# The first microseconds of a linear-attention and SwiGLU kernel: tile 0's mean in two halves on two engines, a split weight load, and a new order of the first tiles

## The chip, the cores and the metric

The kernel runs on one core of a Trainium2 chip. The metric is device time in microseconds (us). The core's engines are TensorE (PE, with its weight loads shown as PEld), VectorE (DVE), ScalarE (ACT), GpSimd (POOL) and SyncE (SP, which here only issues DMAs). Each engine runs its own instructions in order and waits on semaphores for the others.

## The reference

x has 2048 rows of 512 columns in bfloat16. The output is x plus two branches of the same normalised x:

```python
xn = _layernorm(x, axis=-1)                # (x - mean) / sqrt(var + 1e-5), per row
return x + _A_ref(xn, wqkv, wo) + _B_ref(xn, w_gate, w_up, w_down)
# A: q, k, v = xn @ wqkv, 32 heads of 16
#    phi(t) = where(t > 0, t + 1, exp(t)) + 1e-6
#    kv = phi(k)^T v ; z = sum over rows of phi(k)
#    o = phi(q) kv / (phi(q) z + 1e-6) ; o @ wo
# B: (silu(xn @ w_gate) * (xn @ w_up)) @ w_down, 1792 wide
```

## The kernel before, in words

The 2048 rows are 16 tiles of 128 rows (t = 0 to 15). Three stages follow one another on PE: the projections of K and Q with the outer product of xn and phi(K) for all tiles (some 50 us), then the gate and up projections of the feed-forward part with the attention's small matrices between them, then the output tiles.

The order of the work is written out by hand. `K.op(engine, ...)` appends an instruction to an engine's list with the names that it reads and writes; the helper class `_Prog` turns these into semaphore waits. The order of the calls from line 608 on is therefore the order in each engine's queue. DMAs go out on SP's queue (`xload`, L204, tiles of x; `wqkv_load`, L211, blocks of 128 rows of K's or Q's weights, 128 KB each) and two of them on ACT's queue: x of tile 1 and K's block 3.

The head works as follows. PE runs eight matmuls on constants (`fill`, L269) that only keep it busy. For tile 0, DVE takes mean and variance (`bns`, L297, and `agg`, L300), then centres x in two halves of 256 columns (`xc_half`, L380). For tile 1 the mean alone comes from ACT, which copies x times 1/512 with an accumulator (`mean_act`, L305); for tile 2 it comes from `bns` and `agg`. PE transposes the centred blocks of 128 columns (`tp_first`, L408) into PSUM, two to a bank, and ACT copies them to `xcT` (`tc_first`, L420). Then PE projects block by block (`proj_part`, L463, and `proj_first`, L450): a tile's K needs four blocks c of `xcT`, each with the weight block c. Tile 3 is transposed by DMA (`transpose_xc`, L399), tiles 4 and up from xn.

The first tiles are centred but not scaled. The scale 1/sqrt(var+eps) (`rstd`, made on POOL by `eps`, L325, and `rstd_of`, L334) goes in when ACT reads the projections from PSUM: `first_ek` (L520, exponential of K), `first_pk` (L526, positive part of K), `first_pq` (L538, Q). `clip_k` (L503) on DVE and `feat_pool` (L545, POOL) or `first_feat` (L552, DVE) finish phi(K). The outer product `gtacc` (L588) needs phi(K) and xn of the tile; xn comes from DVE (`xn_dve`, L314).

PSUM has eight banks. K of tile t goes to bank 2(t%2), Q to bank 2(t%2)+1, so tile 2 needs tile 0's banks back, and tile 3 those of tile 1: K3 waits for `first_ek(1)` and `first_pk(1)`, Q3 for `first_pq(1)`. The constants' matmuls use bank 3, the transposes of tiles 0 and 1 banks 4 to 7, which `gtacc` takes over.

A matmul's waits are set by the names it reads. One `proj_part` reads one block:

```python
r=[("xcT", t, c // 2), (wname, c)], w=[bk(b)],
```

Of the kernel before, what the change touches and what calls it, by code (L numbers as in the profile page):

```python
# [6 lines left out]
ACT = mybir.ActivationFunctionType  # L7
ALU = mybir.AluOpType
AX = mybir.AxisListType

P = 128
S = 2048
D = 512
# [4 lines left out]
NDC = D // P  # L18
# [90 lines left out]
def bass_parallel_sum__linear_attn_block__swiglu_ffn__prompt_kernel(  # L109
# [12 lines left out]
    K = _Prog()  # L122
    pe, act, dve, pool, sp = nc.tensor, nc.scalar, nc.vector, nc.gpsimd, nc.sync
    bf, f32 = dt.bfloat16, dt.float32

    with contextlib.ExitStack() as es:
        E = es.enter_context

        def sb(name, shape, d=bf):
            return E(nc.sbuf_tensor(name, [P] + shape, d))  # L130

        x_sb = sb("x_sb", [NT, D])
        xn_sb = sb("xn_sb", [NT, D])
        xc_sb = sb("xc_sb", [4, D])
        xcT = sb("xcT", [4 * NDC, P])
# [7 lines left out]
        ident = sb("ident", [P])  # L143
# [3 lines left out]
        mv = sb("mv", [NT, 2], f32)  # L147
        vpe = sb("vpe", [NT], f32)
        rstd = sb("rstd", [NT], f32)
# [4 lines left out]
        warm = sb("warm", [1], f32)  # L154
        mact = sb("mact", [2, 1], f32)
        scr = sb("scr", [D])
        pkq = sb("pkq", [NT, 2, D])
        zacc = sb("zacc", [D], f32)
        zhi = sb("zhi", [D])
# [30 lines left out]
        def bk(i):  # L190
            return ("bank", i)
# [16 lines left out]
        def wqkv_load(eng, h, name, i, c0, n, after=()):  # L208
            K.dma(
                eng,  # L210
                lambda: h.dma_start(  # L211
                    wqkv_sb[:, c0:c0 + n, i * D:(i + 1) * D],
                    A_wqkv[c0 * P:(c0 + n) * P, i * D:(i + 1) * D].rearrange("(c p) f -> p c f", p=P),
                ),
                r=list(after), w=[(name, c) for c in range(c0, c0 + n)],
            )
# [29 lines left out]
        K.op("pool", lambda: pool.memset(nhalf[:, :], -0.5), w=[("nhalf",)])  # L246

        xload("sp", sp, 0, 1)
        wqkv_load("sp", sp, "wk", 1, 0, 2)
        wqkv_load("act", act, "wk", 1, 3, 1)  # L250
        wqkv_load("sp", sp, "wk", 1, 2, 1)
        xload("sp", sp, 2, 1)
# [12 lines left out]
        def fill(n, cols, after=()):  # L265
            K.op(
                "pe",
                [
                    (lambda: pe.matmul(banks[3][:, 0:cols], cw, cx[:, 0:cols], start=True, stop=True))  # L269
                    for _ in range(n)  # L270
                ],
                r=list(after), w=[bk(3)],
            )
# [22 lines left out]
        def bns(t):  # L296
            K.op("dve", lambda: dve.bn_stats(stats[:, t, :], x_sb[:, t, :]), r=[("x", t)], w=[("st", t)])  # L297

        def agg(t):
            K.op("dve", lambda: dve.bn_aggr(mv[:, t, :], stats[:, t, :]), r=[("st", t)], w=[("mv", t)])  # L300

        def mean_act(t):
            K.op(
                "act",
                lambda: act.activation(  # L305
                    scr[:, :], x_sb[:, t, :], ACT.Copy, scale=1.0 / D, accum_out=mact[:, t, :],
                ),
                r=[("x", t)], w=[("mact", t), ("scr",)],
            )

        def xn_dve(t):
            K.op(
                "dve",
                lambda: dve.tensor_scalar(  # L314
                    out=xn_sb[:, t, :], in0=x_sb[:, t, :], scalar1=mv[:, t, 0:1], scalar2=rstd[:, t:t + 1],
                    op0=ALU.subtract, op1=ALU.mult,
                ),
                r=[("x", t), ("mv", t), ("rstd", t)], w=[("xn", t)],
            )

        def eps(t, eng):
            h = dve if eng == "dve" else pool
            K.op(
                eng,
                lambda: h.tensor_scalar(  # L325
                    out=vpe[:, t:t + 1], in0=mv[:, t, 1:2], scalar1=1e-5, scalar2=None, op0=ALU.add,
                ),
                r=[("mv", t)], w=[("vpe", t)],
            )

        def rstd_of(t):
            K.op(
                "pool",
                lambda: pool.tensor_tensor(out=rstd[:, t:t + 1], in0=vpe[:, t:t + 1], in1=nhalf[:, 0:1], op=ALU.pow),  # L334
                r=[("vpe", t), ("nhalf",)], w=[("rstd", t)],
            )
# [35 lines left out]

        HD = D // 2

        def xc_half(t, h, mean=None, dep="mv"):
            mean = mv[:, t, 0:1] if mean is None else mean

            K.op(
                "dve",
                lambda: dve.tensor_scalar(  # L380
                    out=xc_sb[:, t, h * HD:(h + 1) * HD], in0=x_sb[:, t, h * HD:(h + 1) * HD],
                    scalar1=mean, scalar2=None, op0=ALU.subtract,
                ),
                r=[("x", t), (dep, t)], w=[("xc", t, h)],
            )

        def xc_full(t):
            K.op(
                "dve",
                lambda: dve.tensor_scalar(  # L390
                    out=xc_sb[:, t, :], in0=x_sb[:, t, :], scalar1=mv[:, t, 0:1], scalar2=None, op0=ALU.subtract,
                ),
                r=[("x", t), ("mv", t)], w=[("xc", t, 0), ("xc", t, 1)],
            )

        def transpose_xc(t):
# [6 lines left out]
        def tp_first(t, h, b):  # L403
            tb = banks[b].bitcast(bf)[:, 0:HD].rearrange("p (c s) -> p c s", c=2)
            K.op(
                "pe",
                [
                    (lambda c=c: pe.transpose(  # L408
                        tb[:, c, :], xc_sb[:, t, (2 * h + c) * P:(2 * h + c + 1) * P], ident[:, :],
                    ))  # L410
                    for c in range(2)
                ],
                r=[("xc", t, h), ("ident",)], w=[bk(b)],
            )

        def tc_first(t, h, b):
            tb = banks[b].bitcast(bf)[:, 0:HD].rearrange("p (c s) -> p c s", c=2)
            K.op(
                "act",
                lambda: act.activation(xcT[:, NDC * t + 2 * h:NDC * t + 2 * h + 2, :], tb, ACT.Copy),  # L420
                r=[bk(b)], w=[("xcT", t, h)],
            )

        def transpose_dma(t):
# [34 lines left out]
        def proj_part(t, wname, c, pos):  # L459
            lo, b = (D, kb(t)) if wname == "wk" else (0, qb(t))  # L460
            K.op(
                "pe",
                lambda: pe.matmul(  # L463
                    banks[b], xcT[:, NDC * t + c, :], wqkv_sb[:, c, lo:lo + D],
                    start=(pos == 0), stop=(pos == NDC - 1),
                ),
                r=[("xcT", t, c // 2), (wname, c)], w=[bk(b)],
            )

        def kb(t):  # L470
# [47 lines left out]
        def first_ek(t):  # L518
            K.op(
                "act", lambda: act.activation(ek[:, t % NE, :], banks[kb(t)], ACT.Exp, scale=rstd[:, t:t + 1]),  # L520
                r=[bk(kb(t)), ("rstd", t)], w=[("ek", t % NE)],
            )

        def first_pk(t):
            K.op(
                "act", lambda: act.activation(kpos[:, t % NE, :], banks[kb(t)], ACT.Relu, scale=rstd[:, t:t + 1]),  # L526
                r=[bk(kb(t)), ("rstd", t)], w=[("kpos", t % NE)],
            )
# [7 lines left out]
        def first_pq(t):  # L536
            K.op(
                "act", lambda: act.activation(pkq[:, t, 1, :], banks[qb(t)], ACT.Identity, scale=rstd[:, t:t + 1]),  # L538
                r=[bk(qb(t)), ("rstd", t)], w=[("pq", t)],
            )  # L540
# [15 lines left out]
        def clip_k(t):  # L556
            clip(ek[:, t % NE, :], ("ek", t % NE))
# [47 lines left out]
            if t >= 3:  # L605
                transpose_dma(t)

        fill(8, 512)
        bns(0)
        agg(0)  # L610
        xc_half(0, 0)
        xc_half(0, 1)
        mean_act(1)
        xc_half(1, 0, mact[:, 1, :], "mact")
        xc_half(1, 1, mact[:, 1, :], "mact")
        tp_first(0, 0, 4)
        tc_first(0, 0, 4)
        fill(1, P)
        tp_first(0, 1, 5)
        tc_first(0, 1, 5)  # L620
        eps(0, "pool")
        tp_first(1, 0, 6)
        tc_first(1, 0, 6)
        bns(1)
        rstd_of(0)
        xn_dve(0)
        tp_first(1, 1, 7)
        agg(1)
        tc_first(1, 1, 7)
        bns(2)  # L630
        agg(2)
        xc_half(2, 0)
        xc_half(2, 1)
        bns(3)
        agg(3)
        proj_part(0, "wk", 0, 0)
        proj_part(0, "wk", 1, 1)
        proj_part(0, "wk", 3, 2)
        proj_part(0, "wk", 2, 3)
        first_ek(0)  # L640
        clip_k(0)
        xc_full(3)
        bns(4)
        proj_part(1, "wk", 0, 0)
        proj_part(1, "wk", 1, 1)
# [6 lines left out]
        xload("sp", sp, 10, 2)  # L652
        proj_part(0, "wq", 0, 0)
        proj_part(0, "wq", 1, 1)
        first_pk(0)
        tp_first(2, 0, 4)
        tc_first(2, 0, 4)
        tp_first(2, 1, 5)
# [7 lines left out]
        proj_part(1, "wq", 2, 2)  # L666
        proj_part(0, "wq", 3, 3)
        first_pq(0)
        proj_part(1, "wq", 3, 3)
        proj_first(2, "wk", 0)  # L670
        proj_first(2, "wk", 1)
        eps_two(1, "pool")
        rstd_two(1)
        first_ek(1)
        clip_k(1)
        first_pq(1)
        proj_first(2, "wq", 0)
# [7 lines left out]
        xn(4)  # L685
        xload("sp", sp, 12, 2)
        xn_dve(1)
        first_pk(1)
        first_feat(1)
        proj_first(3, "wk", 0)  # L690
        first_ek(2)
# [371 lines left out]
```

## Time and profile before

| | |
|---|---|
| time, median of 3 runs | 211.19 us (210.76 to 211.28) |
| the profiled execution | 211.17 us |
| its span | 209.9 us, 2767 instructions |
| PE busy | 207.3 us, 99% of the span |
| DVE, ACT, POOL busy | 119.5, 70.9, 72.0 us |
| chain that ended last | PE 99% |
| granted TensorE clock | 1.0 |

The span runs from the first to the last instruction of the profiled execution; its own time is 1.27 us longer. Times in the views are counted from the span's start. A line of a timeline gives start and length in us, the engine, the line of the kernel, the operation, what it writes and reads, how many instructions are merged in it, and in brackets how long the engine stood idle before and what ended that. A busy PE is not a PE at its peak: ends of matmuls are modelled and overlap, so the distance between starts tells the rate.

### The profile page before, as it was taken

To read this page: it belongs to the slowest core of one execution; us is meant where nothing else is said; L and a number is where in the kernel's file an instruction comes from. 1 tells how busy PE (TensorE), PEld (TensorE's weight loads), DVE (VectorE), ACT (ScalarE), POOL (GpSimd) and SP (SyncE) were. 2 spreads that over 40 slices of the span, in tenths; PEclk is the share of its full clock that TensorE was granted. 3 is DMA by queue.
4 is the path that set the end of the run, shared out by engine and by line. 5 is a ranking of instruction groups with operands and counts; after the bars stand their busy time and mean duration, and the time that the engine had idled before them with its cause. 6 is when DMAs were issued, how large, how long until landed. Compare 5 with 4: busy or idle time off the path is not lost.

```text
span 209.9 us, 2767 instructions
## 1 busy us (share of the span) xinstructions
PE 207.3 (99%) x987; PEld 95.3 (45%) x987; DVE 119.5 (57%) x245; ACT 70.9 (34%) x125; POOL 72.0 (34%) x90
## 2 busy tenths in 40 slices
PE   8999999999999999999999999999999999999996
PEld 3444444445444444444444444444444444444444
DVE  4989988336265774647365746365556535374122
ACT  5787666966643331302122312213031213121000
POOL 3527977568032444222141432230424032221200
PEclk9999999999999999999999999999999999999999
DMA  6773744894792011110202110202021010210201
GB/s 192 228 192 66 127 100 100 260 365 153 206 352 47 11 28 26 34 25 28 50 2 50 25 28 25 50 0 50 3 50 25 27 25 28 44 33 27 50 25 53
DMA packets 30287, 16.84 MB, mean 80 GB/s; under 512 B 20928, under 2 KB 29632, under 8 KB 30272
## 3 DMA queue, kind: packets, MB, share of 16 engines
q1 hardware_dynamic: 29984, 16.39, 29.6%
q10 hardware_dynamic: 288, 0.26, 0.4%
q8 instruction: 8, 0.13, 0.3%
q14 instruction: 7, 0.06, 0.1%
HBM read 9.70 MB, written 2.10 MB: 56 GB/s over the span
## 4 chain that ended last, share of the span: by engine, by line
PE 99%; DVE 0%; issue 0%
PE psum L783 46%; PE psum L966 23%; PE psum L436 10%; PE psum L955 7%; PE psum L588 7%; PE psum L463 2%; PE psum L269 2%; PE psum L450 2%; PE psum L408 1%; PE psum L881 0%; PE psum L904 0%; DVE out_sb L979 0%
## 5 line engine op out<-in xcount | busy, mean ns | idle before, releaser
L798 ACT ACTIVATE sg<-psum 128x512 bf16<-128x512 f32 x56 | 33.4, 598 | 106.8 <-PE psum L783 104.9
L783 PE MATMUL psum<-xnT,wu_sb 128*128 128x512 bf16 x224 | 57.5, 379 | 0.0
L783 PE MATMUL psum<-xnT,wg_sb 128*128 128x512 bf16 x224 | 57.5, 379 | 0.0
L913 POOL TENSOR_TENSOR prod<-pkq,zb 128x512 f32<-128x512 bf16 x16 | 18.6, 1162 | 57.7 <-DVE pkq L512 57.7
L783 PEld LDWEIGHTS psum<-xnT,wu_sb 128*128 128x128 bf16 x224 | 21.9, 98 | 26.4
L783 PEld LDWEIGHTS psum<-xnT,wg_sb 128*128 128x128 bf16 x224 | 21.9, 98 | 26.2
L979 DVE TENSOR_TENSOR out_sb<-psum,x_sb 128x512 bf16<-128x512 f32 (+2 forms) x17 | 11.2, 660 | 36.3 <-PE psum L966 36.3
L804 DVE TENSOR_TENSOR pkq<-psum,sg 128x512 bf16<-128x512 f32 x28 | 19.2, 687 | 18.5 <-PE psum L783 14.0
L937 POOL TENSOR_TENSOR pqn<-pkq,rden 128x512 bf16<-128x512 bf16 x16 | 16.9, 1057 | 36.6 <-DVE rden L931 36.6
L804 DVE TENSOR_TENSOR xn_sb<-psum,sg 128x512 bf16<-128x512 f32 x28 | 18.8, 673 | 13.8 <-PE psum L783 13.2
L966 PE MATMUL psum<-wd_sb,xn_sb 128*128 128x512 bf16 (+2 forms) x126 | 25.7, 355 | 0.0
L966 PE MATMUL psum<-wd_sb,pkq 128*128 128x512 bf16 x112 | 25.5, 379 | 0.0
L436 PE MATMUL psum<-wqkv_sb,xnT 128*128 128x512 bf16 x96 | 22.5, 379 | 0.0
L580 POOL TENSOR_TENSOR zacc<-zacc,pkq 128x512 f32<-128x512 f32 x15 | 17.3, 1156 | 5.0 <-DVE ek L503 4.6
L966 PEld LDWEIGHTS psum<-wd_sb,xn_sb 128*128 128x128 bf16 x126 | 11.8, 98 | 12.5
L966 PEld LDWEIGHTS psum<-wd_sb,pkq 128*128 128x128 bf16 x112 | 11.0, 98 | 13.2
L955 PE MATMUL psum<-m_sb,eq 128*128 128x512 bf16 (+2 forms) x68 | 16.6, 366 | 0.0
L588 PE MATMUL psum<-pkq,xn_sb 128*128 128x512 bf16 x64 | 15.9, 379 | 0.0
L436 PEld LDWEIGHTS psum<-wqkv_sb,xnT 128*128 128x128 bf16 x96 | 9.4, 98 | 11.3
L921 DVE TENSOR_REDUCE den<-prod 128x32 f32<-128x512 f32 x16 | 10.9, 684 | 5.7 <-POOL prod L913 5.7
L297 DVE BATCH_NORM_STATS2 stats<-x_sb 128x6 f32<-128x512 bf16 x16 | 10.9, 681 | 3.2 <-DMA x_sb<-in_A_x_dram 3.0
L512 DVE SCALAR_TENSOR_TENSOR pkq<-pkq,eq 128x512 bf16<-128x512 bf16 x16 | 11.1, 692 | 0.6
(67 smaller groups left out, 139.6 us busy)
## 6 DMA issues: line engine op xcount, KB each, us to landing
out_dram<-out_sb SPq DMA_DIRECT2D x15, 128.0 KB, 1.7
wg_sb<-in_B_w_gate_dram SPq DMA_DIRECT2D x2, 896.0 KB, 7.8
wu_sb<-in_B_w_up_dram SPq DMA_DIRECT2D x2, 896.0 KB, 6.1
wd_sb<-in_B_w_down_dram SPq DMA_DIRECT2D x1, 1792.0 KB, 9.9
x_sb<-in_A_x_dram SPq DMA_DIRECT2D x5, 256.0 KB, 3.1
x_sb<-in_A_x_dram SPq DMA_DIRECT2D x5, 128.0 KB, 3.5
wqkv_sb<-in_A_wqkv_dram SPq DMA_DIRECT2D x5, 128.0 KB, 3.6
wqkv_sb<-in_A_wqkv_dram SPq DMA_DIRECT2D x1, 512.0 KB, 7.8
```

The costliest lines, as they stand in the source:

```text
L436: (lambda c=c: pe.matmul(banks[b], xnT[:, c, t * P:(t + 1) * P], wqkv_sb[:, c, lo:lo + D], start=(c == 0), stop=(c == NDC - 1),))
L512: lambda: dve.scalar_tensor_tensor(out=dst, in0=src, scalar=0.0, in1=e, op0=ALU.max, op1=ALU.add,),
L580: lambda: pool.tensor_tensor(out=zacc[:, :], in0=zacc[:, :], in1=pk, op=ALU.add),
L588: (lambda c=c: pe.matmul(banks[4 + c], xn_sb[:, t, c * P:(c + 1) * P], pkq[:, t, 0, :], start=(t == 0), stop=(t == NT - 1),))
L783: (lambda c=c: pe.matmul(banks[b], w_sb[:, c, fc * P:(fc + 1) * P], xnT[:, c, C * 512:(C + 1) * 512], start=(c == 0), stop=(c == NDC - 1),))
L798: lambda: act.activation(sg[:, j % NSG, :], banks[gb], ACT.Silu),
L804: lambda: dve.tensor_tensor(out=hT(C, fc), in0=banks[ub], in1=sg[:, j % NSG, :], op=ALU.mult,),
L913: lambda: pool.tensor_tensor(out=p, in0=pkq[:, t, 1, :], in1=zb[:, :], op=ALU.mult),
L937: lambda: pool.tensor_tensor(out=pqn[:, t % NPN, :].rearrange("p (h e) -> p h e", e=DH), in0=pkq[:, t, 1, :].rearrange("p (h e) -> p h e", ...
L955: (lambda g=g: pe.matmul(dst, pqnT(t)[:, g, :], m_sb[:, g, lo:hi], start=(g == 0), stop=False,))
L966: (lambda fc=fc: pe.matmul(dst, hT(C, fc)[:, jj * P:(jj + 1) * P], wd_sb[:, fc, lo:hi], start=False, stop=(fc == NFC - 1),))
L979: lambda: dve.tensor_tensor(out=o, in0=src, in1=x_sb[:, t, lo:hi], op=ALU.add),
```

## The change

Six things change, all in the first part of the order.

1. Tile 0's mean comes from two halves: DVE multiplies columns 0 to 255 by ones and sums them, ACT copies columns 256 to 511 with its accumulator (`mean_parts`). DVE subtracts both parts in one instruction per half tile (`xc_two`). `bns(0)` and `agg(0)` follow behind.
2. The first two transposes of tile 0 go to banks of their own (4 and 1), with a copy of 128 columns each (`tp_quarter`, `tc_quarter`).
3. K's weight blocks 0 and 1 come in two loads of 128 KB instead of one of 256 KB, both on SP.
4. The constants' matmuls are seven of 512 columns, one of 128, and later two of 128 where one was. Tile 1's transposes move behind the first two projections of tile 0.
5. Tiles 1 and 2 are centred in one instruction (`xc_full`). Tile 3's centring moves ahead of `clip_k(0)`.
6. Tile 0 is normalised on ACT (`xn_act`, with a bias from POOL's `negmean`) behind `first_pq(0)`; its eps goes from POOL to DVE; `first_pk(0)` and `first_pk(1)` move up behind `first_ek`.

The core of the diff:

```diff
-        wqkv_load("sp", sp, "wk", 1, 0, 2)
+        wqkv_load("sp", sp, "wk", 1, 0, 1)
+        wqkv_load("sp", sp, "wk", 1, 1, 1)
...
+        def negmean(t):
+            K.op(
+                "pool",
+                lambda: pool.tensor_scalar(
+                    out=nb[:, t:t + 1], in0=mv[:, t, 0:1], scalar1=rstd[:, t:t + 1], scalar2=-1.0,
+                    op0=ALU.mult, op1=ALU.mult,
+                ),
+                r=[("mv", t), ("rstd", t)], w=[("nb", t)],
+            )
+
+        def xn_act(t):
+            K.op(
+                "act",
+                lambda: act.activation(
+                    xn_sb[:, t, :], x_sb[:, t, :], ACT.Identity, scale=rstd[:, t:t + 1], bias=nb[:, t:t + 1],
+                ),
+                r=[("x", t), ("nb", t), ("rstd", t)], w=[("xn", t)],
+            )
...
+        def mean_parts(t):
+            K.op(
+                "dve",
+                lambda: dve.tensor_tensor_reduce(
+                    out=scr2[:, :], in0=x_sb[:, t, 0:HD], in1=cx[:, 0:HD], scale=1.0 / D, scalar=0.0,
+                    op0=ALU.mult, op1=ALU.add, accum_out=mpart[:, 0:1],
+                ),
+                r=[("x", t)], w=[("mpa", t), ("scr2",)],
+            )
+            K.op(
+                "act",
+                lambda: act.activation(
+                    scr[:, 0:HD], x_sb[:, t, HD:D], ACT.Copy, scale=1.0 / D, accum_out=mpart[:, 1:2],
+                ),
+                r=[("x", t)], w=[("mpb", t), ("scr",)],
+            )
+
+        def xc_two(t, h):
             K.op(
                 "dve",
                 lambda: dve.tensor_scalar(
                     out=xc_sb[:, t, h * HD:(h + 1) * HD], in0=x_sb[:, t, h * HD:(h + 1) * HD],
+                    scalar1=mpart[:, 0:1], scalar2=mpart[:, 1:2], op0=ALU.subtract, op1=ALU.subtract,
+                ),
+                r=[("x", t), ("mpa", t), ("mpb", t)], w=[("xc", t, h)],
+            )
...
+        def xct_res(t, c):
+            return ("xcT", 0, "b") if (t, c) == (0, 1) else ("xcT", t, c // 2)
+
+        def tp_quarter(t, c, b):
+            K.op(
+                "pe",
+                lambda: pe.transpose(
+                    banks[b].bitcast(bf)[:, 0:P], xc_sb[:, t, c * P:(c + 1) * P], ident[:, :],
+                ),
+                r=[("xc", t, 0), ("ident",)], w=[bk(b)],
+            )
+
+        def tc_quarter(t, c, b):
+            K.op(
+                "act",
+                lambda: act.activation(xcT[:, NDC * t + c, :], banks[b].bitcast(bf)[:, 0:P], ACT.Copy),
+                r=[bk(b)], w=[xct_res(t, c)],
+            )
...
-        fill(8, 512)
+        fill(7, 512)
+        fill(1, P)
+        mean_parts(0)
+        mean_act(1)
+        xc_two(0, 0)
+        xc_two(0, 1)
         bns(0)
+        xc_full(1, mact[:, 1, :], "mact")
         agg(0)
-        xc_half(0, 0)
-        xc_half(0, 1)
-        mean_act(1)
-        xc_half(1, 0, mact[:, 1, :], "mact")
-        xc_half(1, 1, mact[:, 1, :], "mact")
-        tp_first(0, 0, 4)
-        tc_first(0, 0, 4)
-        fill(1, P)
+        eps(0, "dve")
+        rstd_of(0)
+        negmean(0)
+        tp_quarter(0, 0, 4)
+        tc_quarter(0, 0, 4)
+        tp_quarter(0, 1, 1)
+        tc_quarter(0, 1, 1)
         tp_first(0, 1, 5)
         tc_first(0, 1, 5)
-        eps(0, "pool")
-        tp_first(1, 0, 6)
-        tc_first(1, 0, 6)
+        fill(2, P)
         bns(1)
-        rstd_of(0)
-        xn_dve(0)
-        tp_first(1, 1, 7)
         agg(1)
-        tc_first(1, 1, 7)
         bns(2)
         agg(2)
-        xc_half(2, 0)
-        xc_half(2, 1)
+        xc_full(2)
         bns(3)
         agg(3)
         proj_part(0, "wk", 0, 0)
         proj_part(0, "wk", 1, 1)
+        tp_first(1, 0, 6)
+        tc_first(1, 0, 6)
+        tp_first(1, 1, 7)
+        tc_first(1, 1, 7)
         proj_part(0, "wk", 3, 2)
         proj_part(0, "wk", 2, 3)
+        xc_full(3)
         first_ek(0)
+        first_pk(0)
         clip_k(0)
-        xc_full(3)
         bns(4)
...
-        first_pk(0)
...
         first_pq(0)
+        xn_act(0)
...
         first_ek(1)
+        first_pk(1)
         clip_k(1)
         first_pq(1)
...
-        first_pk(1)
```

More of the change, by code (lines that the diff above doesn't have):

```diff
@@ L156, in bass_parallel_sum__linear_attn_block__swiglu_ffn__prompt_kernel @@
         scr = sb("scr", [D])
+        scr2 = sb("scr2", [D // 2])
+        mpart = sb("mpart", [2], f32)
         pkq = sb("pkq", [NT, 2, D])
@@ L373, in bass_parallel_sum__linear_attn_block__swiglu_ffn__prompt_kernel, with xc_full @@
         HD = D // 2
-        def xc_half(t, h, mean=None, dep="mv"):
+        def mean_parts(t):
[16 more added lines that the diff above has]
+            K.op(
+                "dve",
+                lambda: dve.tensor_scalar(
+                    out=xc_sb[:, t, h * HD:(h + 1) * HD], in0=x_sb[:, t, h * HD:(h + 1) * HD],
+                    scalar1=mpart[:, 0:1], scalar2=mpart[:, 1:2], op0=ALU.subtract, op1=ALU.subtract,
+                ),
+                r=[("x", t), ("mpa", t), ("mpb", t)], w=[("xc", t, h)],
+            )
+        def xc_full(t, mean=None, dep="mv"):
             mean = mv[:, t, 0:1] if mean is None else mean
@@ L380, in xc_half @@
                 lambda: dve.tensor_scalar(
-                    out=xc_sb[:, t, h * HD:(h + 1) * HD], in0=x_sb[:, t, h * HD:(h + 1) * HD],
-                    scalar1=mean, scalar2=None, op0=ALU.subtract,
-                ),
[L384 to L393, printed above, removed]
+                    out=xc_sb[:, t, :], in0=x_sb[:, t, :], scalar1=mean, scalar2=None, op0=ALU.subtract,
+                ),
+                r=[("x", t), (dep, t)], w=[("xc", t, 0), ("xc", t, 1)],
             )
@@ L421, in tc_first @@
                 r=[bk(b)], w=[("xcT", t, h)],
+            )
[10 more added lines that the diff above has]
+        def tc_quarter(t, c, b):
+            K.op(
+                "act",
+                lambda: act.activation(xcT[:, NDC * t + c, :], banks[b].bitcast(bf)[:, 0:P], ACT.Copy),
+                r=[bk(b)], w=[xct_res(t, c)],
             )
@@ L466, in proj_part @@
                 ),
-                r=[("xcT", t, c // 2), (wname, c)], w=[bk(b)],
+                r=[xct_res(t, c), (wname, c)], w=[bk(b)],
             )
```

## The prediction

> **What bounds the kernel now.** I read the page first: TensorE (PE) is busy 99% of the 209.9 us span, and part 4 puts 99% of the chain that ended last on PE. The change touches only the first 13 us, so next I read the chain of waits in order of time, cut to its start (columns: start, length, what).
>
> ```profile
> 0.84 3.57 PE psum L269 x8
> 4.41 0.32 PE psum L408 x2
> 4.73 0.11 PE psum L269
> 4.84 0.64 PE psum L408 x6
> 5.48 2.90 PE psum L463 x12
> 8.37 0.22 PE psum L408 x4
> 8.59 0.86 PE psum L463 x4
> 9.46 1.73 PE psum L450 x8
> ```
>
> The reader sees PE without a gap from the first warming matmul (L269) on. From the first transpose (L408, 4.33) PE does useful work back to back. So a microsecond is won only if this useful work starts earlier or has less to do, and lost wherever PE has to wait.
>
> Second, the spacing of matmuls. 512 columns take 0.427 us before about 6 us (2.93, 3.35, 3.78 in the timeline of L269) and 0.216 after (2.90 us for 12 has one and a half slow ones). The same change shows in the view of line L463:
>
> ```profile
> L463 PE MATMUL psum<-wqkv_sb,xcT x16: 379/379/634, 5.3 to 9.1; 128*128 128x512 bf16 x16
> ```
>
> One matmul of 634 ns is at half rate. The matmuls start at 5.27, 5.70 and 6.05: the second took 0.35, and half rate for x, full rate for 0.35-x, gives 1.2x + 2.4(0.35-x) = 0.512, x = 0.27. So PE stepped to full rate at about 5.97.
>
> Third, the timelines of VectorE (DVE) and ScalarE (ACT) say what releases the first transposes and projections:
>
> ```profile
> 3.04 0.69 DVE L297 BATCH_NORM_STATS2 stats<-x_sb 128x6 f32<-128x512 bf16 x1 [3.04 <-DMA x_sb<-in_A_x_dram]
> 3.77 0.18 DVE L300 BATCH_NORM_AGGREGATE mv<-stats 128x2 f32<-128x6 f32 x1
> 3.99 0.48 DVE L380 TENSOR_SCALAR xc_sb<-x_sb,mv 128x256 bf16<-128x256 bf16 x2
> ...
> 3.35 0.63 ACT L305 ACTIVATE scr<-x_sb 128x512 bf16<-128x512 bf16 x1 [1.05 <-DMA x_sb<-in_A_x_dram]
> 3.88 0.19 ACT L305 ACTIVATION_READ_ACCUMULATOR scr<-x_sb 128x1 f32 x1
> 4.77 1.25 ACT L420 ACTIVATE xcT<-psum 128x256 bf16<-128x256 bf16 x4 [0.69 <-PE psum L408]
> ```
>
> x of tile 0 lands at 3.04, its centred first half starts at 3.99, PE starts on it at 4.33, ACT copies from 4.77 to 5.15, and the first K matmul runs at 5.27.
>
> **The change part by part.**
>
> **1. Mean of tile 0 in halves.** Removed from the path: bn_stats 0.69 + aggregate 0.18 and their gaps, 3.04 to 3.99. Added on ACT: a 256-column copy with accumulator. The 512-column row is 0.629; 256 columns less cost 0.215 on ACT (PSUM copies: 598 and 383 ns), so 0.415, then the accumulator read of 0.186, which starts 0.10 before the end: 3.04+0.415-0.10+0.186 = 3.54. Added on DVE: a reducing two-tensor operation on 256 columns, which no row shows. Two-tensor rows of 128, 384 and 512 columns (L979: 292, 558, 692 ns) give 0.425 for 256. Whether it needs a read of its own is unknown: 0 to 0.186, by ACT's row. At worst the whole is as slow as a 512-wide reduction (L921, 684 ns) plus that read. I take 0.425+0.15, hence 3.61, and 0.04 for the own-engine wait: centring starts at 3.65 (bounds 3.58 and 3.95) instead of 3.99. Its two scalars cost 0.05 more (two-scalar L314 0.400, one-scalar L390 0.347): 0.33. First half ready 3.98, PE 4.04 (4.33 before). The warming matmuls, one of 512 exchanged for one of 128, end at 0.84+7x0.427+0.107 = 3.94, and the identity at 3.84, so neither delays it.
>
> **2. Quarters.** A transpose ends 0.29 after its start and ACT follows 0.04 later: 4.37. A 128-column copy is 0.383-0.107 = 0.276, ending 4.65; from a copy's end to the matmul it was 0.12 (5.15 to 5.27). First K matmul at 4.77, **0.50 earlier**. Second copy ends 4.83, so the second K matmul follows at 5.20, if its weights are there.
>
> **3. What PE does with it.** Tile 1's four transposes, which stood ahead of K0 (4.63 to 5.05), now stand behind its second matmul. Still at half rate: K0's first two 4.77 to 5.62, transposes from 5.62 (0.107 each); the step at 5.97 comes in the fourth; K0's last two 6.02 and 6.23, end 6.45. But the first copy of tile 1 now starts only at 5.73+0.31+0.04 = 6.08 and ends 6.46, so K1 starts at 6.58. Before it was 5.27+0.43+0.35+2x0.216 = 6.48. **The head start of 0.50 is gone: +0.10.** The moved transposes, the half rate and the added 128-column filler eat 0.47 of it (6.45 against 6.48), and the wait for the copy costs 0.13.
>
> On the clock the row comes first: full rate began 5.1 us after the first matmul. The Trainium skill, "TensorE: Matmul & The Clock Gate", Part 1, says PE runs at half rate until about 3.4 us of sustained activity have filled a window that runs free of the kernel. By that rule work moved ahead of the step earns half of its time later, which is against this change; were there no such step, the sum at K1 would be a gain of about 0.2 us. The matmul spacings above agree with it.
>
> **4. K's blocks 0 and 1 in two loads.** One more issue of 0.43 on SP; everything behind it on SP's queue moves: block 2 of K, x of tile 2, four of Q, x of 3 to 7. In the view of DMA issues the loads take longer than they need when alone:
>
> ```profile
> wqkv_sb<-in_A_wqkv_dram SPq DMA_DIRECT2D x1, 256.0 KB, 2.9
> ...
> wqkv_sb<-in_A_wqkv_dram ACTq DMA_DIRECT2D x1, 128.0 KB, 3.7
> ```
>
> 256 KB issued at 1.26 landed at 4.16; x of tile 0, first in line, took 2.2, ACT's block 3 landed at 5.19, SP's block 2 (1.73+3.9) at 5.63, tile 2 (2.23+3.8) at 6.03. DMA busy share is 0.9 to 1.0 from 2 to 7 us, so later issues mostly shorten the queueing: shifts lie between 0 and 0.43. Needed against landing: block 1 at 5.20, issued 1.69, lands 3.9 (+2.2) to 5.2 (block 3's time); I take 4.6. Block 2 at 6.23 against 5.63 to 6.06. Tile 2 at most 6.46; DVE then centres it by 7.75, needed by its transposes at 8.21. Q's first, 2.71+3.6 = 6.3, at most 6.75, needed at 7.34. Cost taken: 0, hidden by these slacks; if block 1 comes with block 2, see rivals.
>
> **5. Tiles 1 and 2 whole, tile 0 normalised on ACT.** One 512-wide centring is 0.347 against 0.48 for two halves: DVE only, off the path. DVE loses 0.40 (L314) and gains 0.15 (eps); bn_stats of tile 0 moves behind centring, so rstd(0) comes at 6.1 instead of 5.1, still ahead of exp of K0 at 6.7. xc(3) and clip(0) swap: clip(0) ends about 9.2, POOL's 1.16 us then gives pk(0) at 10.4, needed by the outer product at 11.02. The added ACT pass (L538's kind, 0.69) ends at 10.56: in time too. But ACT is a full queue here:
>
> ```profile
> 9.28 0.69 ACT L538 ACTIVATE pkq<-psum,rstd 128x512 bf16<-128x512 f32 x1
> 9.87 0.68 ACT L520 ACTIVATE ek<-psum,rstd 128x512 bf16<-128x512 f32 x1
> 10.44 0.69 ACT L538 ACTIVATE pkq<-psum,rstd 128x512 bf16<-128x512 f32 x1
> 11.01 0.70 ACT L526 ACTIVATE kpos<-psum,rstd 128x512 f32<-128x512 f32 x1
> ```
>
> The step is 0.573. With the new pass second, and pk(1) ahead of pq(1), the order is pq0, xn0, ek1, pk1, pq1. pk1, which frees K3's bank, still ends at 11.71, but pq1, which frees Q3's bank, ends at 9.28+4x0.573+0.69 = 12.27, and PE wants that bank at 11.88+2x0.216 = 12.31. With 0.04 to 0.13 from release to matmul, Q3 starts near 12.41: **+0.10**. Behind that ACT has 0.42 of idle time before 13.86, which takes up the remaining 0.57 late by then.
>
> **Sum.** +0.10 (K1) +0.10 (Q3) = +0.20 on the profiled execution (211.17: span 209.9 and 1.27 around it), 0.02 under the median of 211.19. Forecast **211.4**, its own range 211.0 to 211.8. A difference of 0.3%, 0.63 us, is about what a measurement of this kernel can tell from no change.
>
> **Rivals.**
> *The head start survives.* If PE steps to full rate before 4.3, the 0.50 is carried on; if DVE needs no accumulator read, 0.07 more: 210.6. Against it: 5.97 in this execution, and K0's last block lands at 5.63 at the earliest, where K0 ends at 6.48 now. For it: the three times before spread by 0.52, as a step that moves would do. Between, 210.9.
> *Block 1's load is late.* It decides from a landing at 5.15. With block 2's 5.63, the second matmul runs at 5.70 to 6.05, transposes follow, the copy ends at 6.75, K1 starts at 6.87: +0.39, with Q3's 0.10 gives 211.7; with 0.43 more on block 2 of K and tile 2 up to 212.1. For it: block 3 itself took 3.7.
> *Slower by the clock.* PE now idles from 4.68 to 4.77 and, with a late block 1, up to 0.6 us around 5.2. If that gap starts the count to full rate anew, the 5.1 us begin at 5.3 and half rate lasts to 10.4 instead of 5.97: half of 4.4 us is lost, 213.4. It decides at the first gap too long. The gap of 0.07 before 4.33 did no harm. That page's rule, that the window runs free, speaks for 1.7 at most.
>
> **Chances.** Forecast 0.54, head start 0.22, late block 0.16, clock 0.08. Faster by over 0.3% only at the far end of the head start, 0.12; slower: the clock 0.08, half of the late block 0.08, 0.06 of the forecast's high end (a slow reduction and a late tile 2 together): 0.22; the same 0.66. The range 210.6 to 212.2 leaves out the clock and the tails.
>
> **What would show it.** First K matmul near 4.77; ACT's first copy of tile 1 at 6.08; K1 at 6.58; an idle PE before Q3 on ACT's L538; the step to 0.216 near 6. Wrong would be: K1 well under 6.4, a wait of PE on a weight DMA near 5.2, or half rate past 7.

## The result and the profile after

The changed kernel takes 211.43 us (median of 22 runs, 211.04 to 211.77), the kernel before 210.93 (22 runs beside them, 210.49 to 211.56). The ratio is **1.0022, 95% interval 1.0014 to 1.0030**: slower by 0.46 us (0.30 to 0.63). The profiled execution of the changed kernel took 211.42 (span 210.2), that of the kernel before 211.17.

First the chain of waits of the changed kernel, cut to its start (start, length, what). L520 is `proj_part`, L507 `proj_first`, L446 the transposes, L645 `gtacc`, L595 `first_pq`, L327 the new pass for xn, L577 `first_ek`, L583 `first_pk`. K0 stands for the projection of K of tile 0, Q3 for that of Q of tile 3, and so on; K1 "at 6.55" is the start of its first matmul.

```profile
1.72 3.73 DMA wqkv_sb<-in_A_wqkv_dram
5.45 0.14 issue
5.59 0.38 PE psum L520
5.96 0.22 PE psum L446 x4
6.19 2.27 PE psum L520 x10
...
9.36 0.69 ACT pkq L595
10.05 0.70 ACT xn_sb L327
10.75 0.58 ACT ek L577
11.33 0.59 ACT kpos L583
11.92 0.05 issue
11.97 2.04 PE psum L507 x8
14.01 1.73 PE psum L645 x8
```

Before, this chain was PE alone. Now it starts at a weight load: K's block 1, issued on SP at 1.72, lands at 5.45, and the second matmul of K0 waits for it. Later it runs through ScalarE's queue. The eight matmuls from 11.97 (K3 and Q3) take 2.04, where the same number takes 1.73 elsewhere; part of that is how the view merges, and the starts give the wait. The changed kernel, on PE and among PE's weight loads (PEld), then the kernel before:

```profile
11.97 2.04 PE L507 MATMUL psum<-wqkv_sb,xcT 128*128 128x512 bf16 x8
13.85 0.38 PE L645 MATMUL psum<-pkq,xn_sb 128*128 128x512 bf16 x1
12.54 0.98 PEld L507 LDWEIGHTS psum<-wqkv_sb,xcT 128*128 128x128 bf16 x6 [0.47 <-ACT pkq L595]
```

```profile
11.88 1.89 PE L450 MATMUL psum<-wqkv_sb,xcT 128*128 128x512 bf16 x8
13.61 0.38 PE L588 MATMUL psum<-pkq,xn_sb 128*128 128x512 bf16 x1
```

From K3's start to gtacc(1) it is 11.97 to 13.85, 1.88; before it was 11.88 to 13.61, 1.73. So **0.15 is lost before Q3**, whose weight load waits for ScalarE's first_pq(1).

PE's timeline around the first wait:

```profile
4.57 0.61 PE L520 MATMUL psum<-wqkv_sb,xcT 128*128 128x512 bf16 x1
5.59 0.38 PE L520 MATMUL psum<-wqkv_sb,xcT 128*128 128x512 bf16 x1 [0.41 <-DMA wqkv_sb<-in_A_wqkv_dram]
```

The first K matmul runs at 4.57, 0.70 earlier than before; the second at 5.59, 0.11 earlier. K1 starts at 6.55 (6.48 before), K2 at 9.38 (9.29), gtacc(1) at 13.85 (13.61). The distance of 0.23 to 0.24 stays to the end: the last output tile's 14 matmuls start at 207.39 against 207.15.

The head itself, on VectorE and ScalarE:

```profile
2.85 0.42 DVE L400 CUSTOM_DVE_ANT_0 scr<-x_sb,const-bfloat16-1.0 128x256 bf16<-128x256 bf16 x1 [2.85 <-DMA x_sb<-in_A_x_dram]
3.20 0.08 DVE L400 DVE_READ_ACCUMULATOR2_ANT mpart<- 128x1 f32 x1
3.40 0.64 DVE L417 TENSOR_SCALAR xc_sb<-x_sb,mpart 128x256 bf16<-128x256 bf16 x2
```

```profile
2.85 0.42 ACT L408 ACTIVATE scr<-x_sb 128x256 bf16<-128x256 bf16 x1 [0.55 <-DMA x_sb<-in_A_x_dram]
3.17 0.19 ACT L408 ACTIVATION_READ_ACCUMULATOR scr<-x_sb 128x1 f32 x1
...
9.95 0.80 ACT L327 ACTIVATE xn_sb<-x_sb,nb,rstd 128x512 bf16<-128x512 bf16 x1
```

Both halves of the mean are there 0.51 after x lands (x itself was there 0.19 earlier, at 2.85 instead of 3.04; over the profiles below VectorE starts on it between 2.85 and 3.23), and centring starts 0.55 after it, where it took 0.95. The new pass on ScalarE is the longest of its row: it takes 0.80, and its successor starts 0.70 after it, not 0.57.

### The profile page after: what moved, and what is told of

Same layout as the page of the kernel before. It is cut to its first block, busy times and chain, and to the rows that moved or that the text cites. A ratio compares the mean times of both kernels' runs of the same rounds, so it can differ in the third digit from the quotient of the medians.

```text
span 210.2 us, 2760 instructions
## 1 busy us (share of the span) xinstructions
PE 206.1 (98%) x969; PEld 94.9 (45%) x988; DVE 119.8 (57%) x245; ACT 72.0 (34%) x129; POOL 72.0 (34%) x90
## 4 chain that ended last, share of the span: by engine, by line
PE 95%; DMA 2%; ACT 1%; issue 1%; SPq 0%; DVE 0%
PE psum L843 46%; PE psum L1026 23%; PE psum L493 10%; PE psum L1015 6%; PE psum L645 6%; DMA wqkv_sb<-in_A_wqkv_dram 2%; PE psum L520 2%; PE psum L507 1%; PE psum L941 0%; PE psum L964 0%; ACT xn_sb L327 0%; ACT pkq L595 0%; ACT kpos L583 0%; ACT ek L577 0%; PE psum L446 0%
## 5 line engine op out<-in xcount | busy, mean ns | idle before, releaser
L843 PE MATMUL psum<-xnT,wg_sb 128*128 128x512 bf16 x215 | 55.9, 379 | 0.1
L1015 PE MATMUL psum<-m_sb,eq 128*128 128x512 bf16 (+2 forms) x65 | 16.1, 366 | 0.1
L645 PE MATMUL psum<-pkq,xn_sb 128*128 128x512 bf16 x61 | 15.5, 379 | 0.1
```

The costliest lines, as they stand in the source:

```text
L645: (lambda c=c: pe.matmul(banks[4 + c], xn_sb[:, t, c * P:(c + 1) * P], pkq[:, t, 0, :], start=(t == 0), stop=(t == NT - 1),))
L843: (lambda c=c: pe.matmul(banks[b], w_sb[:, c, fc * P:(fc + 1) * P], xnT[:, c, C * 512:(C + 1) * 512], start=(c == 0), stop=(c == NDC - 1),))
L1015: (lambda g=g: pe.matmul(dst, pqnT(t)[:, g, :], m_sb[:, g, lo:hi], start=(g == 0), stop=False,))
```

## The experiments

**Theory and rivals after the result.** Theory: two waits belong to the change, block 1's load near 5.2 and ScalarE's pass before Q3. Rivals: one of them costs nothing by itself; or the difference is only PE's step to full rate, which may fall anywhere. The first two runs undo one part each, the third undoes both, and the fourth puts the split load alone into the kernel before.

**e1: one load for blocks 0 and 1.**

```diff
-        wqkv_load("sp", sp, "wk", 1, 0, 1)
-        wqkv_load("sp", sp, "wk", 1, 1, 1)
+        wqkv_load("sp", sp, "wk", 1, 0, 2)
```

> The changed kernel with K's blocks 0 and 1 in one load of 256 KB again. Theory (two waits: 0.41 us of PE idle on block 1's load near 5.2, and 0.15 us before Q3 on ScalarE): no wait of PE on a weight DMA, second K matmul by 5.2 instead of 5.59, K1 at about 6.40 instead of 6.55, the wait before Q3 stays; 0.15 under the changed kernel, ratio to before about 1.001. Rival (the load costs nothing, because K1 waits for the copy of tile 1 anyway): K1 stays at 6.5 to 6.6, ratio stays at 1.002. Rival (the difference is only the clock's step and the landing of x, which scatter): no order among the kernels, and the ratio anywhere from 0.999 to 1.002.

Measured: ratio to before 1.0002 (0.9992 to 1.0013), an interval that ends just below the changed kernel's. The twelve times fall into two groups, four from 210.72 to 210.87 and eight from 211.17 to 211.59, and the quotient of the medians (211.29 to 211.01) would be 1.0013, so this run alone does not settle what the split costs. PE's timeline and what PE's weight loads waited for between 5 and 6.5 us:

```profile
4.59 0.61 PE L519 MATMUL psum<-wqkv_sb,xcT 128*128 128x512 bf16 x2
5.10 0.40 PE L445 MATMUL psum<-ident,xc_sb 128*128 128x128 bf16 x4
5.33 1.06 PE L519 MATMUL psum<-wqkv_sb,xcT 128*128 128x512 bf16 x3
```

```profile
PEld psum L519 <- DMA wqkv_sb<-in_A_wqkv_dram: 0.4, 1, 0.4
```

K0's first two matmuls now stand together (4.59 and 4.82). In this execution PE was at full rate from the first transpose (4.00) on, and the next limit shows: K0's last matmul stands at 5.79, waiting for block 2 (1.73+4.0 = 5.73). K1 starts at 6.02. The wait on block 1 is gone, and K1 comes earlier than I expected; but part of that is the early step of this execution, which is not the edit's doing (e12 below).

**e2: tile 0 normalised on VectorE again.**

```diff
-        negmean(0)
...
         xc_full(2)
+        xn_dve(0)
...
-        xn_act(0)
```

> The changed kernel with tile 0 normalised on VectorE again, behind the centring of tile 2, and without the two instructions on GpSimd and ScalarE that this replaces. Theory (two waits): K1 as in the changed kernel, 6.55; ScalarE's row ends pq1 0.57 or more earlier, so K3, gtacc(1) and what follows come 0.15 earlier than in the changed kernel (K4 at 15.42 where K1 is at 6.55); ratio to before about 1.001 to 1.0015. Rival (Q3 waits because pk1 stands ahead of pq1, not because of the pass): the wait before Q3 stays, ratio 1.002.

Measured: 1.0014 (1.0004 to 1.0025), the ratio as expected. From K2 to K4 it is 6.12 (9.04 to 15.16), against 6.19 in the changed kernel and 6.05 before. The wait before Q3 is gone (gtacc(1) follows K3 by 1.73), and first_pk(1) still stands ahead of first_pq(1), so the rival falls: it was the pass. But K3 itself now stands 0.08 behind gtacc(0), because the transposing DMA of its tile lands only at 11.58. In the ratio it can't be told from the changed kernel. K0's second matmul runs at 5.13, when block 1 is there (1.72+3.3 = 5.0).

**e3: both edits.**

```diff
-        wqkv_load("sp", sp, "wk", 1, 0, 1)
-        wqkv_load("sp", sp, "wk", 1, 1, 1)
+        wqkv_load("sp", sp, "wk", 1, 0, 2)
...
         xc_full(2)
+        xn_dve(0)
...
-        xn_act(0)
```

> Both of the former edits in the changed kernel. Theory (two waits): no PE idle time on a DMA and none before Q3; K1 at 6.40, 0.08 ahead of the kernel before, and that stays to the end; ratio 0.9995, within 0.999 to 1.0002. Rival (one of the two is no wait of its own): ratio 1.001.

Measured: 1.0005 (0.9995 to 1.0014), above the range of the theory. K1 at 6.05 and no wait before Q3, but a new one:

```profile
11.70 1.89 PE L506 MATMUL psum<-wqkv_sb,xcT 128*128 128x512 bf16 x8 [0.20 <-DMA xcT<-xc_sb]
```

VectorE's pass for xn(0), at 7.43, pushed tile 3's centring to 8.69, and the transposing DMA that follows it, issued at 9.07 (8.67 in e1), lands 2.50 later, at 11.57, when PE already wants K3. The wait was moved, not removed. e3 and e2 ran in the same rounds and differ in the load alone: the medians are 211.09 with one load and 211.50 with two. This pair is the plainest sign that the split costs time, some 0.3 to 0.4 us.

**e4: the kernel before with two loads.**

```diff
-        wqkv_load("sp", sp, "wk", 1, 0, 2)
+        wqkv_load("sp", sp, "wk", 1, 0, 1)
+        wqkv_load("sp", sp, "wk", 1, 1, 1)
```

> The kernel before with only K's blocks 0 and 1 in two loads. Theory (a late block 1 costs only where K0's second matmul would otherwise run sooner): block 1 lands near 5.45, the second matmul runs at 5.6 to 5.7, where it ran anyway; K1 at 6.48 to 6.55; ratio 1.000 to 1.0005. Rival (SP's later issues cost by themselves, through tile 2's x or Q's weights): a wait of VectorE on x of tile 2 or 3 that reaches PE, K2 0.2 or more late, ratio 1.001 or more.

Measured: 1.0006 (0.9997 to 1.0014), between the theory's range and the rival's; block 1 lands near 5.5, K0's second matmul runs at 5.64, K1 at 6.39, K2 to K4 6.04. In a head that runs its second matmul at 5.6 to 5.7 anyway, as this execution's did, the split shows no wait of PE. What it costs in an execution of this kernel with an early step was not seen.

**e5: one load, and VectorE's pass behind clip(0).** Against e3:

```diff
-        xn_dve(0)
...
         clip_k(0)
+        xn_dve(0)
         bns(4)
```

> The changed kernel with one load for K's blocks 0 and 1, and tile 0 normalised on VectorE, now behind clip(0) instead of ahead of tile 3's centring. Theory (the load, ScalarE's pass, and in e3 the transposing DMA of tile 3 that VectorE's pass made late, are three waits, and this has none of them): K1 at 6.0 where the clock steps early and 6.4 where late, K3 right behind gtacc(0), no wait before Q3; ratio 0.9985, within 0.9975 to 0.9995. Rival (the head is bound by the landing of K's block 2 and by the clock, whatever the order): ratio 0.9995 to 1.0005.

Measured: 1.0008 (0.9998 to 1.0019), above the theory's range and nearer to the rival. PE was at half rate until about 6.2 in this execution: first K matmul 4.61, second 5.04, transposes 5.46 to 5.89, and K1 at 6.46, K2 at 9.28, the very place of the kernel before. Nothing waits before Q3; gtacc(1) and (2) together wait 0.13 for VectorE, whose row is later here for two reasons: it has the pass (0.41) in its queue, and at 7.75 it had waited 0.46 for x of tile 3.

**e6: block 3 on SP behind block 1.**

```diff
-        wqkv_load("act", act, "wk", 1, 3, 1)
+        wqkv_load("sp", sp, "wk", 1, 3, 1)
```

> The changed kernel with K's block 3 issued on SP behind block 1 instead of on ScalarE's queue. Theory (block 1 lands late because block 3, issued before it on the other queue, shares the 16 DMA engines with it): block 1 lands by 4.7 instead of 5.45, no PE idle time before the second K matmul; block 3 near 5.2; blocks and x behind it up to 0.45 later; ratio 1.001. Rival (a block issued at 1.7 takes 3.3 to 3.8 whatever shares the engines): block 1 still lands at 5.0 to 5.5, ratio 1.002 or more.

Measured: 1.0034 (1.0021 to 1.0046). DMA issues at 1.75 us, first of the changed kernel (ScalarE's block 3, SP's block 1), then of e6 (block 1):

```profile
wqkv_sb<-in_A_wqkv_dram ACTq DMA_DIRECT2D x1, 128.0 KB, 3.8
wqkv_sb<-in_A_wqkv_dram SPq DMA_DIRECT2D x1, 128.0 KB, 3.7
```

```profile
wqkv_sb<-in_A_wqkv_dram SPq DMA_DIRECT2D x1, 128.0 KB, 2.9
```

Block 1 lands at 4.62 instead of 5.45, **as the theory on the queues has it**. How strongly is less certain, since the landing scatters. With block 3 ahead of it on ScalarE's queue, block 1 landed near 5.5 (changed, e4), at 5.6 (e11), at 5.0 (e2) and at 4.9 (e8, 1.73+3.2):

```profile
wqkv_sb<-in_A_wqkv_dram ACTq DMA_DIRECT2D x1, 128.0 KB, 3.2
wqkv_sb<-in_A_wqkv_dram SPq DMA_DIRECT2D x1, 128.0 KB, 3.2
```

So e6's 4.62 is the earliest of six executions, by 0.3 from the nearest, and it is a single one. The ratio is worse than expected, because another issue on SP is not free at the far end; the chain of e6 shows Q's last block:

```profile
5.07 0.43 SPq L213
5.50 0.04 issue
5.54 3.57 DMA wqkv_sb<-in_A_wqkv_dram
9.12 0.05 issue
9.16 0.60 PE psum L520 x2
```

It was issued at 5.54 and landed at 9.11, and Q0's and Q1's last matmuls wait for it. K2 comes at 9.61.

**e7: the kernel before with only ScalarE's pass** (and first_pk(1) moved up, as in the change).

```diff
-        xn_dve(0)
+        negmean(0)
...
         first_pq(0)
+        xn_act(0)
...
         first_ek(1)
+        first_pk(1)
...
-        first_pk(1)
```

> The kernel before with only tile 0's normalising moved to ScalarE (bias from GpSimd, VectorE's pass left out) and first_pk(1) moved up behind first_ek(1). Theory (ScalarE's queue is full between Q0 and Q3): the start as in the kernel before, K3 at 11.88 where K1 is at 6.48, then 0.1 to 0.2 of wait before Q3, kept to the end; ratio 1.0007. Rival (the wait is the change's head start in another form, which ends at the same place): no wait before Q3, ratio 1.000.

Measured: 1.0016 (1.0004 to 1.0029), above the 1.0007 expected but with it inside the interval, and in the trace K2 to K4 is 6.19 instead of 6.05: the wait stands there without any head start. PE's weight loads of e7:

```profile
12.53 0.98 PEld L469 LDWEIGHTS psum<-wqkv_sb,xcT 128*128 128x128 bf16 x6 [0.46 <-ACT pkq L557]
```

0.15 is what the trace shows; the ratio's 0.34 us has 0.08 to 0.61 as its interval.

**e8: tile 1's transposes first again.**

```diff
+        tp_first(1, 0, 6)
+        tc_first(1, 0, 6)
+        tp_first(1, 1, 7)
+        tc_first(1, 1, 7)
         proj_part(0, "wk", 0, 0)
         proj_part(0, "wk", 1, 1)
-        tp_first(1, 0, 6)
-        tc_first(1, 0, 6)
-        tp_first(1, 1, 7)
-        tc_first(1, 1, 7)
```

> The changed kernel with tile 1's transposes ahead of K0's first two matmuls again, as in the kernel before. Theory (the head start buys nothing while block 1 is late, and the transposes fill that gap): first K matmul at 5.2 to 5.4, second at 5.6, K1 at 6.2 to 6.3 instead of 6.55, no wait for the copy of tile 1; ratio 1.001. Rival (the order of the transposes is indifferent, since K's block 2 and the clock set K1): K1 at 6.5 to 6.6, ratio 1.002.

Measured: 1.0025 (1.0014 to 1.0037), not the 1.001 expected. K1 stands at 6.20 as expected, with the second matmul at 5.55, but with PE at full rate from 4.3 on, and with block 1 there at 4.9, so that in this execution there was no late block for the transposes to cover. The ratio shows no gain over the changed kernel: the order of the transposes made no difference that these runs can tell. Q's weights came late instead: K2 less K1 is 2.87.

**e9: one load, and xn(0) on GpSimd.** Against e1; `xn_pool` is `xn_dve` with GpSimd as its engine:

```diff
         rstd_of(0)
-        negmean(0)
+        xn_pool(0)
...
-        xn_act(0)
```

> The changed kernel with one load for K's blocks 0 and 1, and tile 0 normalised on GpSimd between its scale and the scales of tiles 1 and 2, where GpSimd stood idle for 0.5 to 0.8 us. Theory (the pass for xn of tile 0 costs wherever it meets a full queue, ScalarE's by 0.15, VectorE's by 0.13 to 0.2, and GpSimd's is not full): about 1.06 us on GpSimd by its 512-column rows, from 5.9 to 7.0; no wait before Q3, no wait of K3, of gtacc(1) or gtacc(2); ratio 0.999, within 0.9985 to 1.000. Rival (with one load the pass costs nothing any more; e1 stood at 1.0002): ratio 1.0000 to 1.0005.

Measured: 1.0003 (0.9992 to 1.0015), as the rival has it. GpSimd's pass is twice as long as I took from its other 512-column rows:

```profile
6.14 2.10 POOL L326 TENSOR_SCALAR xn_sb<-x_sb,mv,rstd 128x512 bf16<-128x512 bf16 x1 [0.19 <-POOL rstd L365]
```

No wait before Q3 any more, but 0.14 between gtacc(1) and gtacc(2), for VectorE. K2 to K4 is 6.21.

**e10, e11, e12: the two kernels as they are, looked at again.**

> The kernel before, unchanged, profiled once more. Theory (the clock's step scatters from execution to execution, 4.0 to 6.2 us in the profiles so far, whatever the kernel): the step stands at some other point than 5.97; if it is ahead of 4.5, K1 starts at 6.0 to 6.1, bound by the landing of K's block 2, and the time is near 210.7; if it is behind 5.5, K1 starts at 6.4 to 6.5 and the time is near 211.2. Rival (the step belongs to the order of the work: late in the kernel before, early in the changed one): the step is at 5.8 to 6.2 again.

> The changed kernel, unchanged, profiled once more. Theory (step scatters; block 1's late load and ScalarE's pass belong to the kernel): PE idle on a weight DMA ahead of the second K matmul whenever that is free to run by 5.2, a landing of block 1 between 5.0 and 5.5, and 0.15 before Q3; with an early step also a wait on Q's blocks 2 or 3. Rival (block 1's late landing at 5.45 was one execution's chance): block 1 lands by 4.7, no idle time.

> The kernel before, unchanged, profiled a third time, since all four profiles in its order of work have the clock's step late (5.85 to 6.2), and of nine in the changed order three are at 4.1 to 4.2 and four more between 4.3 and 5.3. Theory (the step scatters in both, and the kernel before's times of 210.5 to 210.9 are executions with an early step): with a time under 210.9 the step stands ahead of 5.0 and K1 starts near 6.0; with a time over 211.0 it is again near 6. Rival (the step comes near 6 always in this order of work): the step near 6 even with a time under 210.9, and what scatters is something else.

e11: block 1 lands at 1.72+3.9 = 5.6, and PE waits for it again (0.44), K1 at 6.69; 0.15 before Q3 again. e10: step near 6.1, 211.31 us, as the rival has it. e12: 210.74 us, and the view of L463 (half-rate matmuls last 634 ns) and its start say why:

```profile
L463 PE MATMUL psum<-wqkv_sb,xcT x16: 379/379/389, 5.2 to 8.6; 128*128 128x512 bf16 x16
```

```profile
5.17 1.04 PE L463 MATMUL psum<-wqkv_sb,xcT 128*128 128x512 bf16 x4
```

No matmul at half rate: the last constants start at 3.35 and 3.64, 0.29 apart, so by the working of the prediction (1.2x + 2.4(0.29-x) = 0.512) the step fell near 3.5. K0 starts no earlier (5.17), but K1 at 6.05. So the step scatters in the kernel before too, and the rival that it belongs to the order of work falls.

All profiles side by side, in us from the span's start. The step is read from the spacing of matmuls; in the changed kernel it falls at the end of K0's first matmul or in the wait behind it. e1 to e9 bear the ratio to the kernel before.

| kernel | step to full rate | K1 | K2 | K2 to K4 | profiled time | ratio (95%) |
|---|---|---|---|---|---|---|
| before | 5.97 | 6.48 | 9.29 | 6.05 | 211.17 | |
| before, e10 | 6.1 | 6.62 | 9.43 | 6.04 | 211.31 | |
| before, e12 | 3.5 | 6.05 | 8.86 | 6.04 | 210.74 | |
| changed | 5.1 to 5.6 | 6.55 | 9.38 | 6.19 | 211.42 | 1.0022 (1.0014, 1.0030) |
| changed, e11 | 5.2 to 5.7 | 6.69 | 9.51 | 6.20 | 211.56 | |
| e1 one load | before 4.0 | 6.02 | 8.83 | 6.19 | 210.86 | 1.0002 (0.9992, 1.0013) |
| e2 xn on VectorE | 4.3 | 6.09 | 9.04 | 6.12 | 211.01 | 1.0014 (1.0004, 1.0025) |
| e3 both | before 4.2 | 6.05 | 8.88 | 6.31 | 211.02 | 1.0005 (0.9995, 1.0014) |
| e4 before, two loads | 5.85 | 6.39 | 9.21 | 6.04 | 211.09 | 1.0006 (0.9997, 1.0014) |
| e5 both, pass later | 6.2 | 6.46 | 9.28 | 6.17 | 211.28 | 1.0008 (0.9998, 1.0019) |
| e6 block 3 on SP | 6.2 | 6.51 | 9.61 | 6.19 | 211.65 | 1.0034 (1.0021, 1.0046) |
| e7 before, pass on ScalarE | 6.2 | 6.56 | 9.37 | 6.19 | 211.41 | 1.0016 (1.0004, 1.0029) |
| e8 tile 1 first | 4.3 | 6.20 | 9.07 | 6.20 | 211.11 | 1.0025 (1.0014, 1.0037) |
| e9 one load, xn on GpSimd | 4.9 | 5.94 | 8.76 | 6.21 | 210.80 | 1.0003 (0.9992, 1.0015) |

The table is read like this: K1 tells what the head was worth, K2 less K1 (2.81 before) whether Q's weights came in time, K2 to K4 what the full queues cost. None of the versions beats the kernel before. With the new head in place, the four versions with one load (e1, e3, e5, e9) stand at 1.0002 to 1.0008, the three with block 1 behind ScalarE's block 3 (changed, e2, e8) at 1.0014 to 1.0025. So within the new head the split load is the larger part of the loss. ScalarE's pass alone, put into the kernel before (e7), is slower clear of noise too; taken out of the new head it gains nothing that the ratios can tell, and in each of its other places PE waits for something else between K2 and K4.

## Why the prediction was right, and where it was wrong

The forecast, 211.4 and slower by about 0.2 us, stands at the measured 211.43, and the change is slower, as forecast. That the level was hit to 0.03 is luck: it was counted from a median of three runs, 211.19, and the kernel before stands at 210.93 in the same rounds. Against that the change costs 0.46 (0.30 to 0.63), so the size was too small, and one step was wrong.

**Step 1, the mean in halves: right.** From x's landing to PE's first transpose I had 1.00 (3.04 to 4.04), measured 1.04 (2.85 to 3.89), before 1.29; in e11 it is 0.96 (3.05 to 4.01). The slower half was ScalarE's, by 0.08, not VectorE's as I had it. The unknown reduction took 0.42 (taken 0.425) and its accumulator read 0.08 (taken 0.15).

**Step 2, the quarters: right.** First K matmul 1.73 after x by the sum, 1.72 measured (1.62 in e11).

**Step 3, K1 at +0.10: right in size by luck, not in its way.** Measured +0.07. The sum let PE work through at half rate and wait for tile 1's copy. Measured, the copy is a wait of about 0.1 (K0 ends at 6.45, K1 starts at 6.55), but what lies ahead of it is block 1's landing, not the half rate. Two terms were off and made up for each other: block 1 came 0.85 later than the 4.6 taken, and the step had come by 5.59 instead of at 5.97, so that the transposes and K0's last matmuls ran at full rate. The statement that the head start comes to nothing holds in both cases, for reasons that replace each other, as versions with one load show: with a late step half rate eats it (e5, K2 at 9.28 against 9.29), with an early one block 2's landing at 5.73 (e1, K1 6.02 against 6.05 of e12).

**Step 4, the split at a cost of 0: wrong.** "I take 4.6" was the failing step: in both profiles of the changed kernel block 1 landed outside the bounds of 3.9 to 5.2 that I gave, at 5.45 and 5.6, and PE waited 0.41 and 0.44 for it. "A wait of PE on a weight DMA near 5.2" was my own sign of being wrong, and it came. In e2 and e8 the same block landed inside the bounds (5.0 and 4.9), still later than 4.6, and in e2 PE waited even so, with an early step. I took the queue as one line with later issues catching up. What the runs point to instead: the block that ScalarE issued 0.23 earlier goes through at the same time, and block 1 lands 0.2 behind it (5.25 and 5.45; 0.2 also in e2, e8 and e11, but 1.0 in e4); with both on SP's queue block 1 lands at 4.62. The Trainium skill, "DMA: Bandwidth & Descriptors", section "Issuing engines are not separate DMA queues", says that DMAs from several engines run on the same 16 DMA engines and interleave; e6 and the changed kernel agree with it. The price on the block that was needed first was 0.83 us between these two profiles, 0.3 between e6 and e8. The late block was a rival with 0.16 and 211.7; its mechanism was the one at work, with a landing at 5.45 instead of 5.63, but its price of 0.39 at K1 did not come, since it left the step at 5.97.

**Step 5, ScalarE's queue: right, the term too small.** 0.15 instead of 0.10. I took first_pq's row (0.69, step 0.573) for the new pass; it takes 0.80 with a step of 0.70. That alone would be 0.13 more; from first_pq's end to Q3's matmul it then took 0.06 (12.48 to 12.54), where the sum had 0.14. The 0.42 of idle time that I set against a delay of 0.57 would not have covered it, but PE lost nothing more: the distance is 0.24 at gtacc(1) and 0.24 in the last output tile. The Trainium skill, "ScalarE: Activation LUTs", section "What ACT_TABLE_LOAD costs", gives 186 ns and 0.833 ns per element, and 93 more for each pointer operand. With both scale and bias as pointers that makes an estimate of 0.80; the trace agrees. The row that I took has one pointer. e7 shows the wait alone.

**The sum.** The two profiled executions differ by 0.25, near the forecast 0.20, and both have a late step. That the medians differ by more fits the scatter of the step: where it comes early the kernel before starts K1 at 6.05 (e12), while a head with the split load has block 1 and Q's weights to wait for (e2, step at 4.3: K2 at 9.04 against 8.86), and the 0.15 on top. e8, which has the split load and ScalarE's pass and a step at 4.3, took 211.11, 0.37 above e12. Of the 22 runs of the kernel before twelve are under 211.0, of the changed kernel's none. But the changed kernel itself was not caught with a step ahead of 5, so this share is argued, not shown.

**The clock.** The prediction held the step at 5.97 as if it were a property of the kernel. In 14 profiles it falls between 3.5 and 6.2, and moves K1 of the kernel before between 6.05 and 6.62. The rival "slower by the clock" did not come: with gaps of 0.41 and 0.44 ahead of the second matmul, that matmul already ran at full rate in both profiles of the changed kernel. The Trainium skill, "TensorE: Matmul & The Clock Gate", Part 1, calls the activity window free-running and the number of slow matmuls variable from run to run; the profiles agree, but with a wider scatter than the 0.5 us either way that it gives.

## What to carry to other kernels

An earlier start is worth only the distance to the next limit: write down the landing of every block that the faster chain will ask for, and the step of the clock, before counting it as a gain. A load split in two let the first half land earlier here (block 0 at 3.5 instead of 4.2), but the second half was issued behind another engine's load and landed later (block 1 at 5.45 instead of 4.2), and all that follows on the queue is issued 0.43 to 0.46 later; look at what is issued between the two. A pass moved to an "idle" engine must be priced at the stretch where it goes, with the row of its own operands: on each of the three engines that it was tried on, PE waited somewhere between K2 and K4 (6.12 to 6.31, where the kernel before took 6.05). And since the step moves K1 by half a microsecond from one execution of the same kernel to the next, a single profile of each version can mislead; compare profiles with the step at the same place, and the times of many runs.

## What the runs showed of the hardware

The table of windows gave a granted clock of 1.00 from 0.8 to 6.0 us in the kernel before, although 512-column matmuls were 0.427 us apart there: the half rate after the start shows in the spacing and the 634 ns matmuls only. GpSimd took 2.10 us for a two-scalar pass over 128x512 (once, in e9), against 1.06 to 1.16 for its two-tensor operations of that size. A DMA issue on SP costs 0.43 to 0.46 of queue, and with two more of them than the kernel before (e6) Q's last block landed at 9.1 us, where 8.0 (4.6+3.4) was the kernel before's and 8.7 (4.6+4.1) the latest with its loads (e7).
